# Divisors of the first batch: from matmuls against the identity to a round trip through DRAM, with the division placed by slot

## Chip, cores, metric

One NeuronCore of a Trainium2 chip. The metric is device time of one execution in microseconds. The kernel before takes 1337.45 us, the median of three runs (1337.2 to 1339.41).

## What is computed

Threshold attention over 8 batches of 8 heads, 576 tokens and head size 64, whose output is the input of a two-layer MLP with an exact GELU, in float32:

```python
scores = scale * np.matmul(q, k.transpose(0, 1, 3, 2))
thresh = np.max(scores, axis=-1, keepdims=True) - tau
scores = np.where(scores >= thresh, scores, -1000000000.0)
scores = scores - np.max(scores, axis=-1, keepdims=True)
attn = np.exp(scores)
attn = attn / (np.sum(attn, axis=-1, keepdims=True) + 1e-09)
...
x = np.ascontiguousarray(attn_out.transpose(0, 2, 1, 3)).reshape(B * S, H * D)
h = x @ w_in                                   # 4608 x 512 by 512 x 2048
g = 0.5 * h * (1.0 + erf(h * inv_sqrt2))
out = g @ w_out                                # 4608 x 2048 by 2048 x 512
```

The kernel does not divide the probabilities. It weighs V with the undivided ones and divides the result x^T (features on partitions, tokens along the row) by the sum of each token's row. The divisor belongs to a token, which is a partition where the sum is made and a column where x^T is divided, so the sums have to be transposed, and repeated over the 64 feature rows of each head. How that is done in the first batch is what the change replaces.

## The kernel before

**Slots.** The order of work is written out by hand: one loop (line 1086) runs over slots `(p, i)`, p a pair of heads, i a chunk of 128 query tokens (i = 4, called NC, is the tail of 64 tokens of both heads together). The first batch is pairs 0 to 3 ("early"), in 20 slots: n = 0 to 7 are chunks 0 and 1 of pairs 0, 1, 2, 3; n = 8 to 10 are chunks 2, 3 and NC of pair 0, n = 11 to 13 those of pair 1, 14 to 16 of pair 2, 17 to 19 of pair 3. From n = 20 (BATCH) on, seven more batches follow with five slots a pair. After them a part on the last ten blocks of 256 tokens ends the program.

**A slot of the first batch** issues, in this order: the scores (TensorE, line 408); `softmax_head`: maxima (VectorE, 420), thresholds `thr` (GpSimd, 423), exponentials (ScalarE, 425); additions of converted weights that have become due (GpSimd, 224); what is due from earlier slots: V weighed (TensorE, 544 or 568; copied to x^T by ScalarE, 554 or 570) and the division; MLP matmuls (`fill`, 636 and 651), as many as a written goal for this slot allows, from n = 10 on; the transposes of the slot before (TensorE 354, copied by ScalarE 361 and 370, for NC 365 and 374); `softmax_tail`: threshold applied and row sums made (VectorE 441). Then come loads and a share of the conversion of the MLP weights (ScalarE 202 and 203, VectorE 210 and 211), which is spread over n = 0 to 19. Each engine carries out its own instructions strictly in that order, so one that waits holds up all behind it. The scores have two PSUM buffers, each free again when line 441 has read it.

**Weights.** They arrive in 32 pieces of 512 KB, issued on the queue of SyncE (SP, line 183). A new piece is issued as a conversion frees a buffer; eight are issued before the first conversion. The SP queue also issues the loads of q, k and v of pairs 4 and 5 (lines 258 and 267) at n = 13 and n = 17. `w_out_sb[15]` to `w_out_sb[12]` are filled by the last four pieces.

**The division in the first batch.** `softmax_tail` gives each slot its own tile of sums, `den`, adds 1e-9 to it on GpSimd (444) and VectorE inverts it a slot later (450). `divide_early`, called right after the V-weighing of the tokens concerned, transposes and repeats the inverses with matmuls: the column of inverses, repeated 64 times, is the stationary side and the identity the moving one (463). ScalarE copies the result out of PSUM (465), and GpSimd multiplies x^T with it (471). It is called eight times: for tokens 0 to 255 of pairs 0 to 3 in n = 3, 5, 7, 9, for tokens 256 to 575 in n = 12, 15, 18, 21. The first MLP matmuls, in n = 10, read tokens 0 to 255 of all four pairs, one pair per value of c, in the order c = 0, 1, 2, 3.

**Later batches** do it otherwise (`divisors`, 473): the sums of a pair stand in the columns of one tile `sums`, are inverted and transposed by VectorE (482), written to DRAM (485) and read back repeated over 64 partitions (491 and 493), and `divide` multiplies (584).

Of the kernel before, what the change touches and what calls it, by code (L numbers as in the profile page):

```python
# [8 lines left out]
FP32 = mybir.dt.float32  # L9
# [3 lines left out]
ALU = mybir.AluOpType  # L13
# [5 lines left out]
def kernel(  # L19
# [40 lines left out]
    TAIL = S - MAIN  # L60
# [4 lines left out]
    N_DF = d_ff // P  # L65
    TOK = 256
# [6 lines left out]
    SLOTS = NC + 1  # L73
# [13 lines left out]
    w_out_sb = [w_out_all[:, j, :] for j in range(N_DF)]  # L87
# [5 lines left out]
    dg = late_end.enter_context(tc.tile_pool(name="dg", bufs=1))  # L93
# [27 lines left out]
    ident = const.tile([P, P], FP32, name="ident")  # L121
# [8 lines left out]
    sums = [att.tile([P, Q], FP32, name=f"sums{i}") for i in range(2)]  # L130
# [111 lines left out]
    st = {}  # L242
# [156 lines left out]
    def scores(p, i):  # L399
        s = st[p]  # L400
        n = 1 if i == NC else 2
        sc = s["sc", i] = [ps.tile([P, 2, 512], FP32, tag="sc", name="sc", bufs=2) for _ in range(n)]
        for h in range(2):
            for e in range(n):
                rows = slice(0, P) if i == NC else slice(e * D, (e + 1) * D)
                lhsT = s["q_tail"] if i == NC else s["qT"][rows, i * P:(i + 1) * P]
                at = h * HALF + (TAIL if p < EARLY and e == 0 else 0)
                nc.tensor.matmul(  # L408
                    sc[e][:, h, 0:HALF], lhsT=lhsT, rhs=s["kT"][rows, at:at + HALF], start=True, stop=True)

    def softmax_head(p, i):

        s = st[p]
        n = len(s["sc", i])
        nmx = small.tile([P, 2], FP32, tag="nmx", name="nmx")
        thr = s["thr", i] = small.tile([P, 2], FP32, tag="thr", name="thr")
        w = s["p", i] = work.tile([P, 2 * S], FP32, tag="p", name="p")
        for e in range(n):
            sc = s["sc", i][e][:, :, 0:HALF]
            nc.vector.tensor_reduce(nmx[:, e:e + 1], sc, axis=AXIS.XY, op=ALU.max, negate=True)  # L420
            if e == 0:
                add_low_bits(True)
            nc.gpsimd.tensor_scalar(  # L423
                thr[:, e:e + 1], nmx[:, e:e + 1], -1.0, tau_eff, op0=ALU.mult, op1=ALU.subtract)
            nc.scalar.activation(  # L425
                w[:, e * S:(e + 1) * S].rearrange("p (h s) -> p h s", h=2), sc, AF.Exp, bias=nmx[:, e:e + 1], scale=1.0)

    def softmax_tail(p, i):

        s = st[p]  # L430
        sc, thr, w = s.pop(("sc", i)), s.pop(("thr", i)), s["p", i]
        n = len(sc)
        if p < EARLY:
            pair = small.tile([P, 2], FP32, tag="den", name="den", bufs=2 * SLOTS)
            den = [pair[:, e:e + 1] for e in range(n)]
        else:
            at = [e * NC + i if i < NC else 2 * NC for e in range(n)]
            den = [sums[p % 2][:, x:x + 1] for x in at]
        for e in range(n):
            row = w[:, e * S:(e + 1) * S].rearrange("p (h s) -> p h s", h=2)  # L440
            nc.vector.scalar_tensor_tensor(  # L441
                row, sc[e][:, :, 0:HALF], thr[:, e:e + 1], row, op0=ALU.is_ge, op1=ALU.mult, accum_out=den[e])
        if p < EARLY:
            nc.gpsimd.tensor_scalar(pair[:, 0:n], pair[:, 0:n], 1e-9, None, op0=ALU.add)
            s["sum", i] = pair[:, 0:n]

    def invert(p, i):

        den = st[p]["sum", i]
        nc.vector.reciprocal(den, den)  # L450

    def divide_early(p, lo, hi):


        s = st[p]
        b, hp = divmod(p, HP)
        tr = ps.tile([P, 512], FP32, tag="mm", name="tr")
        for i in range(lo // P, -(-hi // P)):
            den = s.pop(("sum", i))
            to = tr[:, i * P - lo:min((i + 1) * P, hi) - lo]  # L460
            for e in range(2):
                one_of, cols = (den[:, e:e + 1], ident) if i < NC else (den, ident[:, e * TAIL:(e + 1) * TAIL])
                nc.tensor.matmul(to[e * D:(e + 1) * D, :], lhsT=one_of.to_broadcast([P, D]), rhs=cols, start=True, stop=True)
        by = dg.tile([P, S], FP32, tag="inv", name="inv")
        nc.scalar.copy(by[:, 0:hi - lo], tr[:, 0:hi - lo])
        for n, o, at, size in in_blocks(b, lo, hi):
            x, y = x_blk[n][:, hp, o:o + size], by[:, at - lo:at - lo + size]
            if size == TOK:
                x = x.rearrange("q (p c) -> q c p", c=2)
                y = y.rearrange("q (c p) -> q c p", c=2)  # L470
            nc.gpsimd.tensor_tensor(x, x, y, op=ALU.mult)

    def divisors(p):
# [98 lines left out]
    def in_blocks(b, lo, hi):  # L572
        while lo < hi:
            n, o = divmod(b * S + lo, TOK)
            size = min(TOK - o, hi - lo)
            yield n, o, lo, size
            lo += size
# [498 lines left out]
    PARTS = 1.3, 1.3, 0.2, 1.3, 0.9  # L1076

    HALVED = (2, 3)
    BUSY = {1: 2, 6: 2, 8: 2, BATCH: 4}

    tokens = 0
# [4 lines left out]
    for n in range(len(slots) + WEIGH + 1):  # L1086
        p, i = slots[n] if n < len(slots) else divmod(n, SLOTS)
        early = p < EARLY
        last = slots[n - 1] if 0 < n <= len(slots) else None
        if p < NP:  # L1090
            scores(p, i)
            softmax_head(p, i)
            add_low_bits()
            if last and last[0] < EARLY:
                invert(*last)
            if p < HP - 1 and i == 0:
                turn_qk_early(p + 1)
        elif n == len(slots):
            early_end.close()
            weights_first()  # L1100
# [4 lines left out]
        for args in due:  # L1105
            if len(args) == 2:
                weigh_half(*args)
                if args[1]:
                    divide_early(args[0], 0, TOK)
                continue  # L1110
            weigh_v(*args)
            divide_early(*args)
        due = []
        if p > EARLY and i == WEIGH:
            for lo, hi in (0, WIDE), (WIDE, S):
# [10 lines left out]
        if p < NP:  # L1126
            softmax_tail(p, i)
# [92 lines left out]
```

## Time and profile before

| what | value |
|---|---|
| median of three runs | 1337.45 us |
| the profiled execution's own time | 1338.74 us |
| its span, first to last instruction | 1336.9 us |
| busy: TensorE, VectorE, GpSimd, ScalarE | 99%, 78%, 47%, 45% of the span |
| granted TensorE clock | 0.998 |
| first batch (n = 0 to 19) | up to 127.76 us, where the scores of n = 20 start |
| matmuls of line 463 | 80, 272 ns at the median |
| copies of line 465 | 8, 421 ns at the median |
| reciprocals of line 450 | 20, 155 ns at the median |
| additions of line 444 | 20, 276 ns at the median |
| multiplications of line 471 | 12, 742 ns at the median |

How to read the lines below. A line of the timeline has the start in us from the beginning of the span, the duration in us, the engine (PE is TensorE, PEld its weight load, DVE VectorE, ACT ScalarE, POOL GpSimd, SPq the queue of SyncE), the line of the source, the operation, output and inputs with their shape, and how many instructions were merged; the bracket has the idle time of the engine ahead of it and what ended it. A float32 matmul is two instructions in the trace. Their ends are modelled and overlap by some 0.1 us, so what a group costs TensorE is read from starts: from its first instruction to the start of what follows.

A slot n is found by its scores (line 408). They start at 30.06 (n = 4), 36.14 (5), 41.83 (6), 47.86 (7), 52.48 (8), 59.24 (9), 63.87 (10), 69.04 (11), 74.29 (12), 84.18 (13), 89.28 (14), 93.78 (15), 102.53 (16), 107.63 (17), 113.13 (18), 123.12 (19), 127.76 (20), 131.64 (21) and 141.35 us (22).

### The profile page before, as it was taken

Reading aid. Unit: us, or ns where it says so; the run is one execution under the profiler, and the core shown is the slowest. Engines: PE = TensorE matmul, PEld = TensorE weight load, DVE = VectorE, ACT = ScalarE, POOL = GpSimd, SP = SyncE. Lnnn points to the kernel's source line nnn. Section 1 sums busy time; section 2 is a strip of 40 time slices with the busy share of each in tenths; the row PEclk is TensorE's granted clock in tenths of the full one; section 3 lists DMA queues with packets and bytes.
Section 4 is the critical chain, followed back from the end, with each engine's and each line's share of the span. In section 5 each row is a group of like instructions: output and inputs, shape, how many; then the busy total and the mean of one; then the engine's idle time right before and its main releaser. Section 6 shows DMA issues by size and latency. Waiting matters only on the chain.

```text
span 1336.9 us, 19969 instructions
## 1 busy us (share of the span) xinstructions
PE 1318.9 (99%) x6362; PEld 893.4 (67%) x6362; DVE 1038.9 (78%) x2005; ACT 605.4 (45%) x1029; POOL 633.6 (47%) x1061
## 2 busy tenths in 40 slices
PE   8899999999999999999999999999999999999998
PEld 6677466466466466457556557568787787877877
DVE  6877777788888888888888888783857698386775
ACT  7987457268367358338438438322211113211120
POOL 3655454555555555545546551245264503635530
PEclk9999999999999999999999999999999999999999
DMA  8553566776776786786787775400000130000003
GB/s 258 196 150 62 124 151 141 167 183 153 175 188 153 179 201 153 180 209 155 165 219 164 164 187 124 106 9 1 1 0 1 40 101 18 0 1 0 1 0 79
DMA packets 209784, 152.42 MB, mean 114 GB/s; under 512 B 113360, under 2 KB 193088, under 8 KB 209680
## 3 DMA queue, kind: packets, MB, share of 16 engines
q1 hardware_dynamic: 192256, 127.21, 40.1%
q0 software_dynamic: 16992, 23.64, 6.7%
q8 instruction: 52, 0.85, 0.3%
q14 instruction: 52, 0.43, 0.1%
q10 hardware_dynamic: 432, 0.30, 0.1%
HBM read 55.97 MB, written 12.52 MB: 51 GB/s over the span
## 4 chain that ended last, share of the span: by engine, by line
PE 92%; DVE 2%; ACT 2%; DMA 2%; SPq 1%; issue 1%; POOL 0%; ACTq 0%; DVEq 0%
PE bank L824 34%; PE o_ps L651 17%; PE hT L636 16%; PE sc L408 13%; PE xT L544 11%; ACT p L425 1%; DVE nmx L420 1%; DMA q<-in_q_dram 1%; PE tr L354 1%; DMA x<-xall 1%; DVE power L211 1%; DMA turned_p<-in_moe_w_in_dram 0%; ACT pT L361 0%; DVE p L441 0%; DVE power L210 0%
## 5 line engine op out<-in xcount | busy, mean ns | idle before, releaser
L425 ACT ACTIVATE p<-sc,nmx 128x576 f32<-128x576 f32 x288 | 201.8, 737 | 272.7 <-DVE nmx L420 272.2
L441 DVE SCALAR_TENSOR_TENSOR p<-sc,thr,p 128x576 f32<-128x576 f32 x288 | 225.3, 816 | 74.8 <-ACT p L425 65.1
L423 POOL TENSOR_SCALAR thr<-nmx,tau_eff 128x1 f32<-128x1 f32 x288 | 83.9, 293 | 341.9 <-DVE nmx L420 337.6
L636 PE MATMUL hT<-xall,w_in 128*128 128x256 f32 x1024 | 242.0, 386 | 0.5 <-ACT g L603 0.5
L420 DVE TENSOR_REDUCE nmx<-sc 128x1 f32<-128x576 f32 x288 | 205.4, 750 | 44.5 <-PE sc L408 43.1
L651 PE MATMUL o_ps<-w_out,g 128*128 128x512 f32 x512 | 236.8, 603 | 0.0
L636 PEld LDWEIGHTS hT<-xall,w_in 128*128 128x128 f32 x1024 | 189.3, 190 | 50.8 <-issue 23.0
L706 DVE TENSOR_TENSOR c<-c,bank 128x320 f32<-128x320 f32 x304 | 146.7, 487 | 34.2 <-PE bank L824 21.0
L706 DVE TENSOR_TENSOR o<-o,bank 128x256 f32<-128x256 f32 x240 | 99.8, 419 | 93.7 <-PE bank L824 88.7
L651 PEld LDWEIGHTS o_ps<-w_out,g 128*128 128x128 f32 x512 | 93.1, 190 | 109.2 <-issue 106.8
L408 PE MATMUL sc<-kT,qT 64*128 64x288 f32 x960 | 159.9, 431 | 2.1 <-DVE p L441 1.6
L544 PE MATMUL xT<-pT,v 128*64 128x320 f32 (+1 forms) x1240 | 159.9, 411 | 0.6 <-DVE pT L365 0.5
L505 DVE STREAM_TRANSPOSE turned_p<-p 128x1152 f32<-128x1152 f32 x112 | 154.4, 1378 | 3.9
L408 PEld LDWEIGHTS sc<-kT,qT 64*128 64x128 f32 x960 | 91.0, 186 | 75.8 <-issue 60.1
L544 PEld LDWEIGHTS xT<-pT,v 128*64 128x64 f32 x1240 | 86.7, 137 | 71.9 <-issue 11.3
L824 PE MATMUL bank<-w_out,c 128*128 128x256 f32 x480 | 120.2, 381 | 0.5 <-DVE o L706 0.5
L267 POOL DMA_DIRECT2D v<-in_v_dram x208 | 110.8, 536 | 4.3 <-issue 2.1
L824 PEld LDWEIGHTS bank<-w_out,c 128*128 128x128 f32 x480 | 89.9, 190 | 18.8 <-DVE o L706 3.0
L877 ACT ACTIVATE c<-c 128x320 f32<-128x320 f32 (+1 forms) x80 | 46.9, 623 | 114.6 <-DVE c L706 114.5
L824 PE MATMUL bank<-t_out,c 128*128 128x256 f32 x320 | 82.8, 381 | 0.0
L706 POOL TENSOR_TENSOR c<-c,g 128x320 f32<-128x320 f32 (+1 forms) x40 | 50.5, 1271 | 67.5 <-DVE c L706 67.5
L824 PE MATMUL bank<-t_out,g 128*128 128x256 f32 x320 | 82.1, 379 | 0.0
(180 smaller groups left out, 1757.7 us busy)
## 6 DMA issues: line engine op xcount, KB each, us to landing
pT<-turned_p SPq DMA_DIRECT2D x448, 160.0 KB, 3.5
pT<-pd_tail SPq DMA_DIRECT2D x112, 80.0 KB, 2.7
q<-in_q_dram POOLq DMA_DIRECT2D x104, 72.0 KB, 3.7
k<-in_k_dram POOLq DMA_DIRECT2D x104, 72.0 KB, 3.1
inv<-turned SPq DMA_DIRECT2D x54, 128.0 KB, 4.0
v<-in_v_dram POOLq DMA_DIRECT2D x156, 40.0 KB, 3.1
out_dram<-o SPq DMA_DIRECT2D x40, 128.0 KB, 2.3
xall<-in_moe_w_out_dram SPq DMA_DIRECT2D x9, 512.0 KB, 4.1
```

The costliest lines, as they stand in the source:

```text
L267: eng.dma_start(t[r:P:4, e, 0:n, :], rows[:, r * KR:r * KR + n, :])
L408: nc.tensor.matmul(sc[e][:, h, 0:HALF], lhsT=lhsT, rhs=s["kT"][rows, at:at + HALF], start=True, stop=True)
L420: nc.vector.tensor_reduce(nmx[:, e:e + 1], sc, axis=AXIS.XY, op=ALU.max, negate=True)
L423: nc.gpsimd.tensor_scalar(thr[:, e:e + 1], nmx[:, e:e + 1], -1.0, tau_eff, op0=ALU.mult, op1=ALU.subtract)
L425: nc.scalar.activation(w[:, e * S:(e + 1) * S].rearrange("p (h s) -> p h s", h=2), sc, AF.Exp, bias=nmx[:, e:e + 1], scale=1.0)
L441: nc.vector.scalar_tensor_tensor(row, sc[e][:, :, 0:HALF], thr[:, e:e + 1], row, op0=ALU.is_ge, op1=ALU.mult, accum_out=den[e])
L505: nc.vector.transpose(turned_p[:, :, i // 2, 0:NB, i % 2 * Q:(i % 2 + 1) * Q], w.rearrange("p (e b i) -> p e b i", e=2, i=Q))
L544: nc.tensor.matmul(to, lhsT=s["v"][:, e, c, :], rhs=rhs, start=(c == 0), stop=(c == KR - 1))
L636: nc.tensor.matmul(hT[:, j % 2, :], lhsT=w_in_sb[c][:, j * P:(j + 1) * P], rhs=x_blk[n][:, c, :], start=(c == 0), stop=(c == N_DM - 1))
L651: nc.tensor.matmul(o[:, 0:d_model], lhsT=g[j][:, m * P:(m + 1) * P], rhs=w_out_sb[j], start=(j == 0), stop=(j == N_DF - 1))
L706: eng.tensor_tensor(out, a, b, op=ALU.add)
L824: nc.tensor.matmul(to, lhsT=l, rhs=r, start=start and k == 0, stop=k == len(pairs) - 1, skip_group_check=not start)
```

## The change

The first batch gets its divisors as the later ones do. `softmax_tail` writes the sums of early pairs into columns of `sums[p % 2]` too. After chunk 1 and after NC of a pair GpSimd adds 1e-9 to all nine columns at once. A slot later, at n = 2, 4, 6, 8 (tokens 0 to 255 of pairs 0 to 3) and n = 11, 14, 17, 20 (tokens 256 to 575), the new `divisors_early` inverts the nine columns and transposes the tile on VectorE, writes it to DRAM and reads it back repeated, all on the SP queue. For tokens 0 to 255 the target is `w_out_sb[15 - p]`, which the MLP weights fill later; for the rest it is the tile `inv`, of which there is one. `divide_early` is left with the multiplication on GpSimd. For tokens 256 to 575 it stays where it was (n = 12, 15, 18, 21); for tokens 0 to 255 of pairs 0, 1, 2, 3 it is now in n = 5, 7, 9, 10, after what is due in that slot and ahead of `fill`. Its columns are read in another order (4 x 2 x 32 in place of 2 x 128).

```diff
@@ softmax_tail
-        if p < EARLY:
-            pair = small.tile([P, 2], FP32, tag="den", name="den", bufs=2 * SLOTS)
-            den = [pair[:, e:e + 1] for e in range(n)]
-        else:
-            at = [e * NC + i if i < NC else 2 * NC for e in range(n)]
-            den = [sums[p % 2][:, x:x + 1] for x in at]
+        at = [e * NC + i if i < NC else 2 * NC for e in range(n)]
+        den = [sums[p % 2][:, x:x + 1] for x in at]
...
-        if p < EARLY:
-            nc.gpsimd.tensor_scalar(pair[:, 0:n], pair[:, 0:n], 1e-9, None, op0=ALU.add)
-            s["sum", i] = pair[:, 0:n]
-
-    def invert(p, i):
-        den = st[p]["sum", i]
-        nc.vector.reciprocal(den, den)
+        if p < EARLY and i in (1, NC):
+            at = sums[p % 2][:, 0:2 * NC + 1]
+            nc.gpsimd.tensor_scalar(at, at, 1e-9, None, op0=ALU.add)
+
+    def divisors_early(p, i):
+        den = sums[p % 2]
+        nc.vector.reciprocal(den[:, 0:2 * NC + 1], den[:, 0:2 * NC + 1])
+        turned = small.tile([P, Q], FP32, tag="turned", name="turned", bufs=2)
+        nc.vector.transpose(turned, den)
+        rows = dram.tile([4, Q, Q], FP32, tag="turned", name="turned", bufs=4)
+        nc.sync.dma_start(rows.rearrange("a k i -> (a k) i"), turned)
+        t = w_out_sb[N_DF - 1 - p] if i == 1 else dg.tile([P, S], FP32, tag="inv", name="inv")
+        st[p]["inv", i] = t
+        flat = rows.rearrange("a k i -> a (k i)")
+        c = 0 if i == 1 else 2
+        for e in range(2):
+            to = t[e * D:(e + 1) * D]
+            src = flat[:, (e * NC + c) * Q:(e * NC + c + 2) * Q].unsqueeze(0).to_broadcast([D, 4, 2 * Q])
+            nc.sync.dma_start(to[:, 0:TOK].rearrange("p (a x) -> p a x", x=2 * Q), src)
+            if i == NC:
+                src = rows[2 * e:2 * e + 2, 2 * NC, :].unsqueeze(0).to_broadcast([D, 2, Q])
+                nc.sync.dma_start(to[:, TOK:TOK + TAIL].rearrange("p (a x) -> p a x", x=Q), src)
@@ divide_early
-        tr = ps.tile([P, 512], FP32, tag="mm", name="tr")
-        for i in range(lo // P, -(-hi // P)):
-            den = s.pop(("sum", i))
-            to = tr[:, i * P - lo:min((i + 1) * P, hi) - lo]
-            for e in range(2):
-                one_of, cols = (den[:, e:e + 1], ident) if i < NC else (den, ident[:, e * TAIL:(e + 1) * TAIL])
-                nc.tensor.matmul(to[e * D:(e + 1) * D, :], lhsT=one_of.to_broadcast([P, D]), rhs=cols, start=True, stop=True)
-        by = dg.tile([P, S], FP32, tag="inv", name="inv")
-        nc.scalar.copy(by[:, 0:hi - lo], tr[:, 0:hi - lo])
+        by = st[p].pop(("inv", 1 if lo == 0 else NC))
...
-                x = x.rearrange("q (p c) -> q c p", c=2)
-                y = y.rearrange("q (c p) -> q c p", c=2)
+                x = x.rearrange("q (a i c) -> q a c i", i=Q, c=2)
+                y = y.rearrange("q (a c i) -> q a c i", i=Q, c=2)
             nc.gpsimd.tensor_tensor(x, x, y, op=ALU.mult)
@@ the loop over slots
+    DIVIDE_EARLY = {5: 0, 7: 1, 9: 2, 10: 3}
...
-            if last and last[0] < EARLY:
-                invert(*last)
+            if last and last[0] < EARLY and last[1] in (1, NC):
+                divisors_early(*last)
...
                 weigh_half(*args)
-                if args[1]:
-                    divide_early(args[0], 0, TOK)
                 continue
             weigh_v(*args)
-            divide_early(*args)
+            if args[1]:
+                divide_early(*args)
+        if n in DIVIDE_EARLY:
+            divide_early(DIVIDE_EARLY[n], 0, TOK)
         due = []
```

More of the change, by code (lines that the diff above doesn't have):

```diff
@@ L442, in softmax_tail @@
                 row, sc[e][:, :, 0:HALF], thr[:, e:e + 1], row, op0=ALU.is_ge, op1=ALU.mult, accum_out=den[e])
-        if p < EARLY:
-            nc.gpsimd.tensor_scalar(pair[:, 0:n], pair[:, 0:n], 1e-9, None, op0=ALU.add)
-            s["sum", i] = pair[:, 0:n]
-    def invert(p, i):
-        den = st[p]["sum", i]
-        nc.vector.reciprocal(den, den)
+        if p < EARLY and i in (1, NC):
[19 more added lines that the diff above has]
+                nc.sync.dma_start(to[:, TOK:TOK + TAIL].rearrange("p (a x) -> p a x", x=Q), src)
     def divide_early(p, lo, hi):
-        s = st[p]
         b, hp = divmod(p, HP)
-        tr = ps.tile([P, 512], FP32, tag="mm", name="tr")
-        for i in range(lo // P, -(-hi // P)):
-            den = s.pop(("sum", i))
-            to = tr[:, i * P - lo:min((i + 1) * P, hi) - lo]
-            for e in range(2):
-                one_of, cols = (den[:, e:e + 1], ident) if i < NC else (den, ident[:, e * TAIL:(e + 1) * TAIL])
-                nc.tensor.matmul(to[e * D:(e + 1) * D, :], lhsT=one_of.to_broadcast([P, D]), rhs=cols, start=True, stop=True)
-        by = dg.tile([P, S], FP32, tag="inv", name="inv")
-        nc.scalar.copy(by[:, 0:hi - lo], tr[:, 0:hi - lo])
+        by = st[p].pop(("inv", 1 if lo == 0 else NC))
         for n, o, at, size in in_blocks(b, lo, hi):
```

## The prediction

> **What bounds the kernel now.** I began with the page's chain that ended last: TensorE holds 92% of it. Then a table by stage (columns: stretch, its length, busy us and instruction count of PE, PEld, DVE, ACT, POOL, granted clock, DMA share, GB/s) shows where that isn't so.
>
> ```profile
> PE 92%; DVE 2%; ACT 2%; DMA 2%; SPq 1%; issue 1%; POOL 0%; ACTq 0%; DVEq 0%
> ```
>
> ```profile
> 0.00:64.00 64.00, 55.37 (x504) 40.78 (x505) 47.92 (x113) 52.57 (x110) 30.88 (x56) 0.97 0.73 233
> ...
> 113.00:123.00 10.00, 9.25 (x62) 6.18 (x63) 7.42 (x17) 7.23 (x17) 5.27 (x10) 1.00 0.14 31
> ...
> 141.50:160.00 18.50, 18.50 (x60) 8.90 (x61) 14.90 (x28) 4.13 (x7) 11.69 (x24) 1.00 0.71 157
> ```
>
> Up to 64 us TensorE has 8.6 us of idle time, so its work there is not simply the bound; in n = 10 to 21 it is nearly so; from n = 22 on it never idles. A shift gained or lost by 141 us therefore goes through to the end. All of the change lies ahead of that. So the timeline of n = 9 to 17 was read next, for who waits for whom.
>
> ```profile
> 61.56 0.61 PE L463 MATMUL tr<-ident,den 128*64 128x128 f32 x8
> ...
> 64.41 0.74 POOL L471 TENSOR_TENSOR xall<-xall,inv 128x256 f32<-128x256 f32 x1
> ...
> 64.95 3.19 PE L636 MATMUL hT<-xall,w_in 128*128 128x256 f32 x14
> ...
> 66.24 1.27 POOL L224 TENSOR_TENSOR w_in<-power,w_in 128x512 uint32<-128x512 uint32 x1 [0.72 <-DVE power L211]
> ...
> 67.49 0.30 POOL L423 TENSOR_SCALAR thr<-nmx,tau_eff 128x1 f32<-128x1 f32 x1
> ...
> 68.61 1.07 ACT L361 COPY pT<-tr 128x512 f32<-128x512 f32 x2 [1.00 <-PE tr L354]
> ```
>
> See that GpSimd finishes pair 3's division at 65.15, 1.1 us ahead of its first use: the fourth MLP matmul, at 64.95 + 3 x 0.43 = 66.24 (pitch 0.43: seven from 64.95 to 67.97). And that ScalarE waits for TensorE's transposes right after.
>
> ```profile
> 102.24 1.07 ACT L361 COPY pT<-tr 128x512 f32<-128x512 f32 x2 [2.17 <-PE tr L354]
> ...
> 105.38 1.27 POOL L224 TENSOR_TENSOR w_out<-power,w_out 128x512 uint32<-128x512 uint32 x1 [3.34 <-DVE power L211]
> ...
> 106.63 0.30 POOL L423 TENSOR_SCALAR thr<-nmx,tau_eff 128x1 f32<-128x1 f32 x1
> ...
> 106.96 0.82 DVE L441 SCALAR_TENSOR_TENSOR p<-sc,thr,p 128x576 f32<-128x576 f32 x1 [0.99 <-POOL thr L423]
> ...
> 107.63 1.45 PE L408 MATMUL sc<-pd_tail,qT 64*128 64x288 f32 x8
> ```
>
> Here, in n = 16 and 17, VectorE waits for a GpSimd threshold, and TensorE's scores for VectorE (107.71, end of the first part of line 441). GpSimd itself had idled 3.34 us. Last, the SP queue, and what divisors through DRAM cost in later batches:
>
> ```profile
> 86.46 0.33 SPq L183 DMA_DIRECT2D xall<-in_moe_w_out_dram  x1
> 86.84 2.13 SPq L258 DMA_DIRECT2D q<-in_q_dram  x4
> 89.14 3.08 SPq L258 DMA_DIRECT2D k<-in_k_dram  x4
> 92.33 5.03 SPq L267 DMA_DIRECT2D v<-in_v_dram  x8
> 97.46 0.52 SPq L183 DMA_DIRECT2D turned_p<-in_moe_w_out_dram  x1
> ...
> 164.56 0.57 SPq L485 DMA_DIRECT2D turned<-turned  x1
> 166.57 0.60 SPq L491 DMA_DIRECT2D inv<-turned  x1
> ```
>
> SP is taken up for 11 us in n = 13 to 15 by pair 4's loads; and the reading back is issued 2.0 us after the writing.
>
> [...] 16 KB to DRAM lands after 1.9 us at the median (1.8 to 2.9), the reads after 3.9 (3.4 to 5.7, line 491). [...] of two 512 KB pieces issued 0.63 us apart (97.46, 98.09) one lands after 4.0 us, the other after 5.0. [...] line 210 takes 0.96 us at 64.47 in place of 0.42 while line 471 runs. [...]
>
> **The change, part by part.** Signed costs on the path, in us.
>
> *TensorE.* 80 matmuls go. From first start to what follows, four groups take 0.54 each (61.56 to 62.10 in n = 9; n = 3, 5, 7 alike), four 0.65 to 0.9 (78.91 to 79.56 in n = 12; n = 15, 18, 21). *ScalarE* loses eight copies of 0.42.
> - n = 3: line 361 starts at 29.68, waiting for TensorE. Without line 463 (28.56 to 29.00) and line 465, it can start when line 554 (from 28.69, 0.40) and four transposes are done, 29.25: **-0.43**. n = 5: likewise 41.44 to 40.91, **-0.53**.
> - n = 7 and 9: **0**. VectorE's chain is unbroken from 43.3 to 67: line 211 ends (49.87), line 224 takes 1.27 from 50.02, then thr, then line 441 at 51.60, 1.8 us in every slot.
> - n = 12: TensorE is on the path (ScalarE waits 3.06 for it): **-0.65**. n = 15 the same: **-0.65**.
> - n = 18: TensorE idles 0.45 for ScalarE's line 603. The built program now makes these matmuls wait on TensorE alone, since a PSUM tile fewer is in turn; the next bound is line 603's end at 120.6, for transposes that started at 121.62. I take **-0.6** (0 to -1.0).
> - n = 21: scores of n = 22 start at 141.35; VectorE's line 441 frees the second of their two buffers at 141.09, and the second of four matmuls (0.29 each) needs it, so they start near 140.8: **-0.5**.
>
> *VectorE.* 20 reciprocals go, 8 and 8 transposes (0.21, line 482) come. The pair takes 0.37 and fits into the 0.48 us ahead of line 441 in which it waits for thr anyway; in n = 14 and 20 it overhangs by 0.1, under slack of 0.3 and 0.5. **0**. *GpSimd* makes 12 additions fewer, none on the path; the new column order of the multiplication is not in the trace: 0.74, at most 1.0 each. **0**, 0.26 above in n = 10.
>
> *Weights behind the new SP traffic.* SP stands 2 to 5 us at each write. Pieces land 8 us or more ahead of use after the first six (piece 9: issued 26.9, used 47.7), so **0**; without that cover each us would be a us. Pair 4's loads are ahead of it; pair 5's move from 102 to about 119 and are used at 140.6.
>
> *Division of pair 3 in n = 10.* It now stands behind line 224 and thr of that slot: start 67.77, end 68.5, and the fourth MLP matmul waits for it from 66.24. Queued behind: three MLP matmuls, the transposes, ScalarE's copies, line 202, line 210, maxima of n = 11. All that was tight (ScalarE waited 1.00). **+2.35** (2.3 to 2.6). The other three are done where or before the old ones were.
>
> *Division of pair 1, tokens 256 on, in n = 15.* By then the sum is +0.74 (n = 13). Its five DMAs stand behind pair 4's 16 loads and a 512 KB piece: write issued at 98.05 + 0.74 = 98.8. [...] it lands near 102.0, after 3.2 us. The reads go out at 102.1, 102.7, 103.4, 104.0; the third, the last that the larger multiplication needs, lands at 107.3, the fourth at 107.9. Multiplications end at 108.4 (0.74 and 0.32), line 224 at 109.7, thr at 110.0. Without that, thr would end at 106.93 + 0.09 = 107.0. VectorE's line 441 and TensorE's scores of n = 17 wait: **+3.0**. Lower bound: 1.9 to land and 3.4 to read, 1.1. Upper: reads of 5.9, 4.8. Pair 0's reads (n = 12) land near 83, GpSimd's next work is at 87; pairs 2 and 3 (n = 18, 21) are in before their turn.
>
> Sum: -0.43 - 0.53 + 2.35 - 0.65 - 0.65 + 3.0 - 0.6 - 0.5 = **+2.0**. The profiled execution (span 1336.9, own time 1338.74) would become 1338.9 and 1340.7; it lies 1.29 above the median of the runs, to which I apply the same +2.0: **1339.4**.
>
> **Rivals.** A measurement can tell about 0.2%, 2.7 us, from no change.
> 1. *Main case*: both waits, second one 1.1 to 3.7: 1337.5 to 1340.1. Chance 0.45.
> 2. *Slower*: the reads for pair 1 land past 108.7; from there the sum exceeds 2.7. For it: a piece in front, [...] landings of up to 5.9 seen. Against: nothing issued behind them. At 4.8 it gives 1341.2. Chance 0.33.
> 3. *Second wait absent*: needs the reads in by 104.4, sooner than any seen: -1.0, 1336.4. Chance 0.05.
> 4. *Faster*: the first is covered too, or taken up by idle time of TensorE in n = 12 to 18 (0.67, 0.29, 0.24, 0.45): 1336.4 - 2.35 = 1334.1. Against: these gaps are ends of chains through TensorE itself. Chance 0.12.
> 5. *It doesn't do what it says*: SP's stops starve the conversion after all; some 3 us more than case 1, 1342.4. Chance 0.05.
>
> Faster by over 0.2% has 0.12 (case 4), slower 0.38 (2 and 5), within it 0.50. The range leaves out case 5, most of case 4 and the top of 2: 1335.5 to 1341.6; the main case's own is 1337.5 to 1340.1.
>
> **What would show it.** Line 463 gone; in n = 10 a TensorE gap of 2.3 us ended by GpSimd's multiplication; in n = 15 GpSimd idle until a DMA, and VectorE's wait for thr in n = 16 grown from 1.0 to about 4; scores of n = 22 starting near 143.3. It is wrong if either gap is missing, if ScalarE waits for a weight piece, or if line 441 waits in n = 12, 18 or 21.

## Result and the profile after

The changed kernel takes **1351.99 us**, the median of four runs (1351.79 to 1354.53); the kernel before takes 1337.38 (four runs). The ratio is 1.0116, its 95% interval 1.0103 to 1.0129. The profiled execution has a span of 1350.1 us, 13.2 more than before. The forecast was 1339.4, its range ended at 1341.6. (A single run can fall into a slower state of the chip: one of the 13 of the last experiment took 1512.13 us at a granted clock of 0.85 and is left out of its median.)

The page's chain that ended last, after the change. TensorE had 92% of it before and has 88% now; DMA has gone from 2% to 4%:

```profile
PE 88%; DMA 4%; DVE 3%; SPq 2%; ACT 1%; issue 1%; POOL 1%; DVEq 0%; ACTq 0%; POOLq 0%
```

The table by stage of the changed kernel (columns as before the change: stretch, its length, busy us and instruction count of PE, PEld, DVE, ACT, POOL, granted clock, DMA share, GB/s):

```profile
64.00:80.00 16.00, 6.68 (x24) 5.28 (x22) 3.49 (x7) 1.64 (x3) 2.52 (x4) 0.69 0.47 169
...
153.50:172.00 18.50, 18.50 (x60) 8.89 (x58) 14.90 (x28) 4.80 (x7) 12.30 (x24) 1.00 0.67 143
```

Of the kernel before, the stretch of the first row:

```profile
64.00:80.00 16.00, 15.31 (x94) 11.24 (x95) 13.53 (x29) 13.37 (x29) 9.38 (x15) 1.00 0.56 170
```

This is the news: in 64 to 80 us TensorE works 6.68 us in place of 15.31, and its clock is at 0.69 in place of 1.00. The last row of the changed kernel is n = 22, in which TensorE is full as it was. So the loss lies ahead of it. To place it, the start of each slot's scores (line 408) was compared, after minus before:

| slot n | 2 | 4 | 6 | 10 | 11 | 12 | 13 | 15 | 16 | 17 | 18 | 19 | 21 | 22 | 24 on |
|---|---|---|---|---|---|---|---|---|---|---|---|---|---|---|---|
| shift, us | -0.56 | -1.08 | -1.52 | -1.06 | +11.22 | +11.09 | +10.53 | +10.54 | +10.02 | +10.02 | +13.59 | +13.04 | +13.07 | +12.53 | +12.9 |

Two steps lose much: n = 10 to 11, **+12.28**, and n = 17 to 18, **+3.57**. (n = 2, 9 and 22 lose some 0.36 each.) The timeline of n = 10 after the change:

```profile
63.25 0.75 POOL L476 TENSOR_TENSOR xall<-xall,w_out 128x256 f32<-128x256 f32 x1
63.85 1.46 PE L641 MATMUL hT<-xall,w_in 128*128 128x256 f32 x6
65.15 1.26 POOL L224 TENSOR_TENSOR w_in<-power,w_in 128x512 uint32<-128x512 uint32 x1 [1.15 <-DVE power L211]
66.39 0.29 POOL L423 TENSOR_SCALAR thr<-nmx,tau_eff 128x1 f32<-128x1 f32 x1
...
73.84 0.73 POOL L476 TENSOR_TENSOR xall<-xall,w_out 128x256 f32<-128x256 f32 x1 [7.16 <-DMA w_out<-turned]
74.63 3.78 PE L641 MATMUL hT<-xall,w_in 128*128 128x256 f32 x8 [9.32 <-POOL xall L476]
78.20 2.13 PE L354 MATMUL tr<-ident,p 128*128 128x128 f32 x9
```

GpSimd is through with line 224 and the threshold at 66.7, as forecast, and then waits 7.16 us for a DMA: pair 3's divisors. TensorE waits 9.32 us for GpSimd. (Matmuls are counted here and below by their instructions in the trace, two to a matmul of the source; a transpose is one. So the 80 of line 463 are 40 matmuls of the source.) Then its eight matmuls take 3.78 us and nine transposes 2.13; the same take 1.99 and 1.15 where the clock is at 1.00 (kernel with division first, below). 9.32 + 1.79 + 0.98 is 12.1 of the 12.28.

Why the divisors are late is told by SP's queue in the changed kernel (line 453 is the write, 461 the reads, 183 a piece of weights):

```profile
46.67 0.54 SPq L183 DMA_DIRECT2D turned_p<-in_moe_w_in_dram  x1
47.32 0.37 SPq L183 DMA_DIRECT2D xall<-in_moe_w_in_dram  x1
47.82 0.35 SPq L183 DMA_DIRECT2D turned_p<-in_moe_w_in_dram  x1
48.27 0.77 SPq L453 DMA_DIRECT2D turned<-turned  x1
55.58 1.25 SPq L461 DMA_DIRECT2D w_out<-turned  x2
56.94 0.54 SPq L183 DMA_DIRECT2D xall<-in_moe_w_out_dram  x1
57.58 0.37 SPq L183 DMA_DIRECT2D turned_p<-in_moe_w_out_dram  x1
58.05 0.37 SPq L183 DMA_DIRECT2D xall<-in_moe_w_out_dram  x1
58.53 0.40 SPq L183 DMA_DIRECT2D turned_p<-in_moe_w_out_dram  x1
59.02 0.60 SPq L453 DMA_DIRECT2D turned<-turned  x1
67.57 1.25 SPq L461 DMA_DIRECT2D w_out<-turned  x2
```

SP stands from a write until it lands, since the reads behind it need it: pair 3's lands at 67.56, its reads go out at 67.57. Meanwhile conversions free buffers, and when SP is let go, three pieces, then four go out in a row, some 0.5 us apart. The kernel before sent them two to a slot here, 1.05 us apart or more:

```profile
54.83 0.33 SPq L183 DMA_DIRECT2D xall<-in_moe_w_out_dram  x1
55.89 0.33 SPq L183 DMA_DIRECT2D turned_p<-in_moe_w_out_dram  x1
60.28 0.33 SPq L183 DMA_DIRECT2D xall<-in_moe_w_out_dram  x1
61.33 0.33 SPq L183 DMA_DIRECT2D turned_p<-in_moe_w_out_dram  x1
```

Pair 3's write is issued right behind its four pieces and lands after 8.5 us, 0.17 us after the last of them. From write to reads it is 5.5, 4.8, 7.3, 8.5 us for pairs 0 to 3.

The second loss, n = 15 to 17 after the change:

```profile
116.67 1.02 POOL L476 TENSOR_TENSOR xall<-xall,inv 128x256 f32<-128x256 f32 x2 [6.16 <-DMA inv<-turned]
117.65 1.27 POOL L224 TENSOR_TENSOR w_out<-power,w_out 128x512 uint32<-128x512 uint32 x1
118.90 0.30 POOL L423 TENSOR_SCALAR thr<-nmx,tau_eff 128x1 f32<-128x1 f32 x1
119.23 0.82 DVE L437 SCALAR_TENSOR_TENSOR p<-sc,thr,p 128x576 f32<-128x576 f32 x1 [3.31 <-POOL thr L423]
120.11 1.23 PE L408 MATMUL sc<-pd_tail,qT 64*128 64x288 f32 x6 [1.71 <-DVE p L437]
121.27 4.97 PE L641 MATMUL hT<-xall,w_in 128*128 128x256 f32 x14
```

GpSimd's order holds its next work up: the threshold's maxima are there at 115.91, but it starts at 118.90, behind the wait of 6.16 us and line 224. This is the forecast chain, but its last row isn't: 14 matmuls of the MLP take 4.97 us, and took 3.29 before.

### The profile page after: what moved, and what is told of

It is laid out like the page before. It is cut to its first block, busy times and chain, and to the rows that moved or that the text cites. A ratio compares the mean times of both kernels' runs of the same rounds, so it can differ in the third digit from the quotient of the medians.

```text
span 1350.1 us, 19850 instructions
## 1 busy us (share of the span) xinstructions
PE 1321.2 (98%) x6282; PEld 893.1 (66%) x6282; DVE 1039.2 (77%) x2001; ACT 603.5 (45%) x1021; POOL 629.5 (47%) x1049
## 3 DMA queue, kind: packets, MB, share of 16 engines
q0 software_dynamic: 16992, 23.64, 6.8%
## 4 chain that ended last, share of the span: by engine, by line
PE 88%; DMA 4%; DVE 3%; SPq 2%; ACT 1%; issue 1%; POOL 1%; DVEq 0%; ACTq 0%; POOLq 0%
PE bank L829 34%; PE o_ps L656 16%; PE hT L641 15%; PE sc L408 12%; PE xT L549 10%; DMA turned<-turned 1%; PE tr L354 1%; DVE p L437 1%; DMA x<-xall 1%; DVE nmx L420 1%; ACT p L425 1%; DMA turned_p<-in_moe_w_in_dram 0%; DMA w_out<-turned 0%; DVE power L210 0%; DVE power L211 0%
## 5 line engine op out<-in xcount | busy, mean ns | idle before, releaser
L641 PE MATMUL hT<-xall,w_in 128*128 128x256 f32 x1024 | 245.5, 389 | 9.3 <-POOL xall L476 9.3
L711 POOL TENSOR_TENSOR c<-c,g 128x320 f32<-128x320 f32 (+1 forms) x40 | 50.5, 1272 | 67.5 <-DVE c L711 67.5
```

The lines of the kernel that those rows point to most:

```text
L641: nc.tensor.matmul(hT[:, j % 2, :], lhsT=w_in_sb[c][:, j * P:(j + 1) * P], rhs=x_blk[n][:, c, :], start=(c == 0), stop=(c == N_DM - 1))
L711: eng.tensor_tensor(out, a, b, op=ALU.add)
```

## Experiments

Three theories were put to the test. **Theory 1**: SP, held at each landing, lets freed pieces pile up, and the next write lands behind their burst. **Theory 2**: the way through DRAM is long in itself. **Theory 3**: the place of pair 3's division in GpSimd's order decides. "Step" is the growth of the shift against the kernel before from the start of one slot's scores to the next; it is cleaner than the total (see the end of this part). Every kernel starts from the changed one unless said otherwise; its line numbers differ from the changed kernel's by what the edit adds.

**Reads a slot later.** The write stays, the first half's reads are issued in the next slot.

```diff
         nc.sync.dma_start(rows.rearrange("a k i -> (a k) i"), turned)
+        st[p]["rows"] = rows
+        if i == NC:
+            read_divisors(p, i)
+
+    def read_divisors(p, i):
+        rows = st[p].pop("rows")
...
+            if n > 1 and slots[n - 2][0] < EARLY and slots[n - 2][1] == 1:
+                read_divisors(*slots[n - 2])
```

> The changed kernel, but the reads of the first half's divisors are issued one slot after the write, so that SP doesn't stand still at the write's landing. Theory 1 (SP held at each landing lets freed pieces pile up, and the next write lands behind their burst): the pieces go out singly, each write lands in some 2 to 4 us, pair 3's reads are in by 66, the wait of n = 10 shrinks from 9.3 us to about 2 (the division still stands behind GpSimd's other work), total about 1342. Theory 2 (the way through DRAM is long in itself): the reads come a slot later still, the wait of n = 10 stays at 9 us or grows, total 1352 or more. Theory 3 (where the division stands in GpSimd's order decides): unchanged, 1352.

Measured: 1343.29 us, ratio 1.0047 (1.0032 to 1.0062). The step of n = 10 falls from 12.28 to 4.04. Its timeline (write 453, reads 467, division 482):

```profile
57.10 0.33 SPq L453 DMA_DIRECT2D turned<-turned  x1
...
59.81 0.33 SPq L183 DMA_DIRECT2D xall<-in_moe_w_out_dram  x1
...
60.87 0.33 SPq L183 DMA_DIRECT2D turned_p<-in_moe_w_out_dram  x1
...
61.28 1.25 SPq L467 DMA_DIRECT2D w_out<-turned  x2
...
67.71 0.73 POOL L482 TENSOR_TENSOR xall<-xall,w_out 128x256 f32<-128x256 f32 x1
...
68.49 3.67 PE L647 MATMUL hT<-xall,w_in 128*128 128x256 f32 x8 [2.12 <-POOL xall L482]
```

The pieces go out no more than two in a row again, and pair 3's write lands after 3.1 us (8.5). The reads, a slot later in the order, go out 6.3 us earlier (61.28, not 67.57). Theories 2 and 3 fall as the main cause. (SP is not quite free: for pairs 1 and 2 it still stands at the landing, after 6.3 and 4.9 us, but then no burst of three or four follows.) Of the step left, 2.12 us are the wait for a division that starts right behind the threshold, 1.9 us after its reads have landed; the other 1.7 us are the eight matmuls, 3.67 in place of 1.99.

**Reads without a wait.** The first half's reads take a tile of ones written at the start, so SP is never held by these writes; tokens 0 to 255 of the first batch are divided by wrong numbers.

```diff
+        if i == 1:
+            rows = ones_rows
```

> The changed kernel, but the reads for tokens 0 to 255 take a DRAM tile of ones that was written once at the start, so they don't wait for the write just ahead of them; the writes stay. Left out: tokens 0 to 255 of the first batch are divided by the wrong numbers. All instructions and transfers are otherwise the same. Theory 1: SP is never held, no bursts, wait of n = 10 about 2 us, total about 1341 to 1342. Theory 2, if it is the reads that are slow: 1350 or more; if it is the landing of the write: as theory 1, but pieces bunched as now. Theory 3: 1352.

Measured: 1345.21 us, ratio 1.0061 (1.0046 to 1.0076); step of n = 10 4.05, again a wait of 2.12 us and eight matmuls in 3.63. The instructions and bytes are those of the changed kernel but for the one write of the ones, yet the reads wait for no landing: 8.2 us of the 12.28 go with that. This kernel takes away the whole wait for the landing, and not only SP's hold; that it is the hold is shown by the kernel with the reads a slot later, whose divisors do come through DRAM and whose step is the same (4.04). The total is 3 to 4 us above its expectation: the eight slow matmuls weren't in it (1.7), and the step of n = 17 is 5.26 in place of 3.57 (see the second half).

**The write on ScalarE's queue.**

```diff
-        nc.sync.dma_start(rows.rearrange("a k i -> (a k) i"), turned)
+        (nc.scalar if i == 1 else nc.sync).dma_start(rows.rearrange("a k i -> (a k) i"), turned)
```

> The changed kernel, but the first half's writes are issued by ScalarE into its own queue; the reads stay with SP. Theory 1: [...] lands in 2 to 3 us, so SP is held shortly and the wait of n = 10 falls to 2 to 5 us; against it stand four issues on ScalarE of about 0.4 us each: total 1342 to 1346. If the pieces slow the write by sharing the DMA engines and DRAM [...], the write still takes 5 us or more and the total stays near 1350. Theory 3: 1352 or more.

Measured: 1349.77 us, ratio 1.0100 (1.0083 to 1.0117). For pair 3 it is 3.4 us from write (63.59) to reads (67.01), and the step of n = 10 is **2.36**; the forecast was 2.35. The expectation of the total was wrong, for another reason: the step of n = 2 is +6.0.

```profile
74.97 1.99 PE L641 MATMUL hT<-xall,w_in 128*128 128x256 f32 x8 [2.12 <-POOL xall L476]
```

```profile
26.96 0.35 ACTq L453 DMA_DIRECT2D turned<-turned  x1
27.36 0.69 ACT L327 ACTIVATE qT<-tr,q_scale 128x512 f32<-128x512 f32 x1 [5.36 <-DMA xall<-in_moe_w_in_dram]
28.09 0.93 PEld L354 LDWEIGHTS tr<-ident,p 128*128 128x128 f32 x5 [7.25 <-ACT qT L327]
```

ScalarE itself stood 5.36 us at the issue until a piece had landed. The semaphores in the trace explain it: in this program the DMAs of SP and ScalarE take eight in turn, and the write waits for the DMA that had the same one eight issues before, a piece issued at 22.46 and landed at 26.88. Moving a DMA to a busy engine's queue moved such a wait there too.

**SP held again, all else repaired.** The reads are issued at the end of the slot of the write, ahead of that slot's new pieces, pair 3's division stands first in n = 10, and the second half's division a slot later.

```diff
-            if n > 1 and slots[n - 2][0] < EARLY and slots[n - 2][1] == 1:
-                read_divisors(*slots[n - 2])
...
+        if last and last[0] < EARLY and last[1] == 1:
+            read_divisors(*last)
```

> All divisors through DRAM, with three repairs: the first half's reads are issued at the end of the slot in which the write is issued (ahead of that slot's new pieces), pair 3's division stands first in n = 10, and the second half's division for pairs 0 to 2 stands one slot later. If the three causes found are all there is, no step loses more than 0.4 and the gains remain (n = 5 -0.44, n = 12, 15, 18, 21 together -2.2): about 1334.5, 3 us below the kernel before. If holding SP at the landing in itself brings the bursts back, n = 10 costs several us again and the total is 1340 or more.

Measured: 1346.27 us, ratio 1.0066 (1.0051 to 1.0080). It was meant as the best version, and the case named last in its expectation came: writes take 5.9, 7.1 and 7.9 us again, the step of n = 10 is 7.83.

```profile
53.34 0.54 SPq L183 DMA_DIRECT2D xall<-in_moe_w_out_dram  x1
53.98 0.37 SPq L183 DMA_DIRECT2D turned_p<-in_moe_w_out_dram  x1
54.45 0.38 SPq L183 DMA_DIRECT2D xall<-in_moe_w_out_dram  x1
54.93 0.37 SPq L183 DMA_DIRECT2D turned_p<-in_moe_w_out_dram  x1
56.23 0.33 SPq L453 DMA_DIRECT2D turned<-turned  x1
64.13 1.25 SPq L467 DMA_DIRECT2D w_out<-turned  x2
```

Reads moved by less than a slot bring the burst of four and the late landing back. Theory 1 holds in both directions.

**The bursts alone.** Only the second half is divided by way of DRAM; the first half's writes and reads are issued, but TensorE turns its divisors as before the change.

```diff
-                invert(*last)
+                divisors_early(*last)
...
     def divisors_early(p, i):
+        if i == 1:
+            invert(p, i)
```

(Shown against the kernel with the second half alone, below. `invert` keeps a copy of the inverted sums, which TensorE then turns; what the DMAs bring is not used.)

> The kernel with only the second half through DRAM (+2.27 us at n = 22 by its profile, +3.9 by its median), and the first half's writes and reads issued as in the changed kernel, but not used: TensorE turns these divisors as before. Left out is nothing of the computation. SP is held at each landing and the pieces come in bursts. If the conversion of the weights has the slack that the prediction gave it (0 for this step), n = 10 costs nothing and no step differs by more than 0.5 from the kernel without these transfers: 1338 to 1342. If the held pieces starve the conversion, ScalarE waits for them and some slots up to n = 12 lose 1 us or more each.

Measured: 1344.80 us, ratio 1.0054 (1.0035 to 1.0073). SP's queue shows the same bursts (57.98 to 59.57, write 60.03, reads 67.88), and n = 10 and 11 lose nothing by them: their steps are 0.00 and 0.01. So the conversion of the weights has the slack the prediction gave it. (n = 14 and 15 together lose 0.56 against the kernel with the second half alone; why stays open.) The total is above the expected range; by the slots the kernel is at +3.6 until 584 us, and the rest (5.5, in the profiled execution) comes between 585 and 710 us, which this part's end takes up.

**Division first.** On the kernel with the reads a slot later, pair 3's division is moved ahead of line 224 and the threshold in n = 10.

```diff
+        if n == 10:
+            divide_early(3, 0, TOK)
         if p < NP:
             scores(p, i)
...
-        if n in DIVIDE_EARLY:
+        if n in DIVIDE_EARLY and n < 10:
```

> The kernel with the reads a slot later, and pair 3's division placed first among GpSimd's work of n = 10 (ahead of that slot's line 224 and threshold) instead of last. With the reads a slot later, the step from n = 10 to 11 cost 4.04: a wait of 2.12 us for the multiplication and 1.8 us in which eight MLP matmuls ran at 0.50 of the clock. If the place of the division in GpSimd's order is what is left (the term of +2.35), the wait falls to the arrival of the reads (issued 61.28 and 61.9, landing after 4.1, so near 66.0, multiplied by 66.8, needed at 66.4): 0.4 us or less, no fall of the clock, step of 0 to +0.6, and the time falls by 3.5 to 4. If the reads are what is late, the step stays at 3 to 4.

Measured: 1342.12 us, ratio 1.0033 (1.0021 to 1.0045); step 1.71 in place of 4.04. Half a hit: the place in GpSimd's order matters, but then the reads are what ends last. They land near 66.6, not 66.0, and TensorE waits 1.47 us, with no fall of the clock:

```profile
66.75 0.74 POOL L482 TENSOR_TENSOR xall<-xall,w_out 128x256 f32<-128x256 f32 x1 [2.00 <-DMA w_out<-turned]
...
67.54 1.99 PE L647 MATMUL hT<-xall,w_in 128*128 128x256 f32 x8 [1.47 <-POOL xall L482]
69.37 1.15 PE L354 MATMUL tr<-ident,p 128*128 128x128 f32 x9
```

Theory 3 names part of what is left behind theory 1; the last 1.5 us are theory 2's, the length of the way itself.

**TensorE kept busy.** On the same kernel, 16 matmuls of no use stand ahead of the matmul that waits.

```diff
+                if n == 0 and j == 0 and c == 3:
+                    keep_busy(4)
```

> The kernel with the reads a slot later, and 16 matmuls of no use (about 2.3 us) ahead of the fourth MLP matmul of n = 10, so that TensorE is not idle while it waits for pair 3's division. If the fall of the clock after a wait is a cost of its own, the clock stays at 1.00, the eight matmuls behind the wait take 1.85 us in place of 3.67, and the step from n = 10 to 11 falls from 4.04 to about 2.4. If those matmuls are slow for another reason (operands, DMA traffic), the step stays at 4 or grows by what the filling exceeds the wait.

Measured: 1345.29 us, ratio 1.0054 (1.0038 to 1.0069). The total did not fall (1343.29 without the filling), but the step did what was expected, 2.37 in place of 4.04:

```profile
66.18 1.95 PE L304 MATMUL idle<-ident 128*128 128x128 f32 x16
...
68.47 1.99 PE L649 MATMUL hT<-xall,w_in 128*128 128x256 f32 x8 [0.35 <-POOL xall L482]
```

The division ends at the same time as without the filling (68.4), and the eight matmuls take 1.99 us in place of 3.67. The fall of the clock is a cost of its own, 1.7 us here.

**Second half alone, and pair 1's place in SP's queue.** First only tokens 256 on go through DRAM.

```diff
-            if last and last[0] < EARLY and last[1] in (1, NC):
+            if last and last[0] < EARLY and last[1] == 1:
+                invert(*last)
+            if last and last[0] < EARLY and last[1] == NC:
                 divisors_early(*last)
```

> Only tokens 256 on go through DRAM; tokens 0 to 255 are turned by TensorE and copied by ScalarE where they were before. All three theories put the 12.3 us of n = 10 on the first half, so it must go; the steps of n = 12, 15, 16/17, 18 and 21 must stay as in the changed kernel (-0.56, -0.52, +3.57, -0.55, -0.54, together +1.4): 1338.8 us, 1.4 above the kernel before. If the time stays near 1352, or lies below 1337, the steps don't add up and the shift by slot is no sum of causes.

Measured: 1341.51 us (12 runs, 1337.61 to 1345.05), ratio 1.0025 (1.0015 to 1.0035). The 12.28 go, n = 12, 15, 18 and 21 keep their gains (-0.56, -0.52, -0.55, -0.54); n = 17 costs 5.06 in place of 3.57. There the clock falls for longer, 6.8 us in place of 3.4: six matmuls of the scores take 2.28 us (1.23 in the changed kernel) behind a wait of 2.04. The run with the clock at 1.000 in the mean is the one of 1337.61, the one at 0.996 that of 1345.05.

Two repairs of this kernel. Division of pairs 0 to 2 a slot later:

```diff
             weigh_v(*args)
+            if args[1] and args[0] < EARLY - 1:
+                then.append(args)
+                continue
             divide_early(*args)
```

(`then` is worked off in the next slot behind the exponentials and additions of weights.)

> Only tokens 256 on go through DRAM, and the division for pairs 0 to 2 stands one slot later in GpSimd's order (pair 3's where it was). If the cost of n = 15 to 17 is the wait of GpSimd for the reads with line 224 and the threshold of n = 16 queued behind (measured 5.06 us with its fall of the clock in the kernel with only this half), it goes altogether; the gains of n = 12, 15, 18 and 21 (-0.56, -0.52, -0.55, -0.54) remain: 2 to 3 us below the kernel before, 1335.0. If the wait moves on with the division to n = 17 or 18, the time stays near 1340.

Measured: 1340.38 us, ratio 1.0016 (1.0005 to 1.0027). GpSimd no longer waits for the reads and the step of n = 17 is 0.71, but n = 14 costs 0.40 and in n = 15 the gain of -0.52 becomes +0.08, presumably since the multiplications now stand in GpSimd's way a slot later. Most of the cost goes, not all of it. The total missed the 1335 expected; this profile's scores of n = 0 start 1.7 us late, too. And pair 4's 16 loads behind pair 1's divisors:

```diff
-        if p == 1 and i == NC:
-            load(HP)
...
                 divisors_early(*last)
+            if last == (1, NC):
+                load(HP)
```

> Only tokens 256 on go through DRAM, as in the kernel with only this half (whose steps n = 15 to 17 cost 5.06 net), and SP issues pair 4's 16 loads behind the divisors of pair 1 instead of ahead of them. If those divisors are late because they queue behind the loads, they arrive before n = 15 needs them, the wait of GpSimd (6 us) goes, the 5.06 goes, and n = 12, 15, 18 and 21 keep their -0.5 each: 2 to 3 us below the kernel before, 1335, unless pair 4's q is now late for its scaling in n = 17. If the way through DRAM is late without the loads too, at least 1 to 3 us of the 5.06 stay and the time is 1337 or more.

```profile
91.65 0.33 SPq L459 DMA_DIRECT2D turned<-turned  x1
93.48 0.59 SPq L467 DMA_DIRECT2D inv<-turned  x1
...
96.08 2.21 SPq L258 DMA_DIRECT2D q<-in_q_dram  x4
```

Measured: 1337.53 us, ratio 1.0001 (0.9993 to 1.0009). From write to reads it is 1.8 us, GpSimd multiplies at 99.22 without a wait, and the step of n = 17 is 0.16. So pair 1's divisors were late because they stood behind the loads and the piece. The total is 2.5 us above the 1335 expected, though by the slots this kernel is at -2.0 us from n = 24 on (-0.5 of it ahead of n = 0).

**All repairs together.** The edits of three kernels above, in one: reads a slot later, pair 3's division first, loads behind pair 1's divisors; all divisors through DRAM.

> All divisors through DRAM, reads of the first half a slot later, pair 3's division first in n = 10 (together 1.71 left of 12.28 at that step), and pair 4's loads behind pair 1's divisors. If the three causes are separate, the step at n = 16 and 17 (3.94 there) goes as well: from 1342.1 to about 1338.3, level with the kernel before. If one repair undoes another, it stays above 1340.

Measured: 1336.55 us (12 runs), ratio 0.9995 (0.9987 to 1.0003). Steps of 1.22 in n = 10 and 0.02 in n = 17: the causes are separate. And with pair 3's first half left to TensorE, in the old place of its division:

```diff
-            if last and last[0] < EARLY and last[1] in (1, NC):
+            if last == (EARLY - 1, 1):
+                invert(*last)
+            elif last and last[0] < EARLY and last[1] in (1, NC):
                 divisors_early(*last)
...
                 weigh_half(*args)
+                if args == (EARLY - 1, 1):
+                    divide_early(args[0], 0, TOK)
...
-        if n in DIVIDE_EARLY:
+        if n in DIVIDE_EARLY and n < 10:
```

> Divisors through DRAM except for pair 3's first half, which TensorE turns as before; first half's reads a slot later; pair 4's loads behind pair 1's divisors. By the causes found no wait is left: n = 10 costs 0, n = 16 and 17 cost 0, and the gains of n = 5 (-0.44), 12, 15, 18 and 21 (-0.5 to -0.56 each) remain: 1334.5 to 1335.5, about 2.5 us below the kernel before. If it lies above 1337.4, a cost was overlooked that the other kernels hid.

Measured: 1337.27 us (12 runs), ratio 0.9997 (0.9989 to 1.0005); steps 0.38 and 0.00. The 1335 expected was missed. By the slots these two are at -3.1 and -2.2 us from n = 24 on, of which -0.9 and 0.0 lie ahead of n = 0 already; in the total neither can be told from the kernel before. Their profiles, one execution each, lose 1.0 and 1.4 us of it between 585 and 755 us. **What stays open**: there TensorE's wait differs from profile to profile. Near 590 us, where ScalarE waits for a buffer that is being written to DRAM (3.94 us in the kernel before), TensorE waits 1.07 us in the kernel before, 2.06 and 1.68 in these two, and 2.34 in the kernel with the bursts alone, there followed by 3.4 us at half the clock. Whether a shift of the first batch changes these waits in the mean was not tried. The kernel before alone spreads from 1334.8 to 1340.7 in 35 runs.

## Why the prediction was wrong, point by point

- **"Division of pair 3 in n = 10", +2.35: the step that failed; measured 12.28.** It took line 224 and the threshold as all that the division waits for. With the reads in time just that is measured (2.36 in the kernel with the write on ScalarE's queue, the same wait of 2.12 in two others). The landing of these reads was never worked out, though it was for pair 1's in n = 15. Ready 56.03, written 59.02, landed 67.5, read 67.57 to 68.8, used 73.84: the same sum, with 3.0 us until the write is issued and 8.5 until it lands, gives the wait. Moving the reads a slot later, so that no burst stands ahead of the write, took 8.2 of the 12.28 away.
- **"Weights behind the new SP traffic", 0**: true of the weights (bursts alone: n = 10 and 11 lose nothing). But "SP stands 2 to 5 us at each write" was too small (4.8 to 8.5), and the question stopped at who waits for the pieces. It had to go on: what do pieces that are held back collide with when they are let go? With the next write. Rival 5 named SP's stops, but had the conversion starve; the divisors did.
- **TensorE's clock, nothing charged for it**: wrong. It is 2.8 us of n = 10 and 1.7 of n = 17. That waits such as those forecast cost no clock was the author's estimate, and the trace before already spoke against it: its clock is at 0.50 from 23.64 to 27.05 us, and TensorE's only wait in the 3.4 us ahead of that took 1.53 us (21.1 to 22.6). Half clock came behind a wait of 2.12 us in two kernels and not in a third; the last part sets them side by side.
- **"Division of pair 1, tokens 256 on, in n = 15", +3.0; measured 3.57**: mechanism right, terms not. The write to reads took 3.3 us (forecast 3.2, the author's estimate; the write landed at 111.81, the piece ahead of it at 111.60), third read to multiplication 3.5 (3.9), so the threshold ended 2.25 us late, not 3.0, and TensorE lost 1.9 of the 3.57 by the wait; 1.7 are the clock (14 matmuls in 4.97 us, not 3.29). VectorE's wait for the threshold grew from 0.99 to 3.31 us (forecast: about 4). Two errors that nearly cancel: that 3.57 lies near 3.0 is luck. Its cause, the loads ahead in SP's queue, is shown by their move.
- **n = 12, 15, 18, 21** (-0.65, -0.65, -0.6, -0.5): -0.56, -0.52, -0.55, -0.54. But of the last, 0.37 is given back in n = 22: its scores start earlier and then take 1.54 us in place of 1.17, up to the next matmul, the second of their buffers being free no sooner. All 13 kernels that have the change, whole or in part, show these 0.37. **n = 5** (-0.53): -0.44, and 0.00 in the kernel that keeps TensorE's turn in n = 5. **n = 7 and 9** (0): +0.10 and +0.35; the latter is there without the first half's change too, unexplained. **n = 3** (-0.43): n = 2 and 3 together show -0.52. The kernel with the second half alone, which keeps these matmuls, shows -0.97, but only because its clock doesn't fall near 24 us, as it does in the kernel before and in the changed one. Like against like, the matmuls are worth 0.4: with the fall, -0.03 where they are kept (two kernels) and -0.41 to -0.52 where they are gone (five); without it, -0.97 to -0.99 (two) and -1.40 to -1.43 (three). The forecast holds.
- **VectorE and GpSimd, 0**: right; the multiplication in its new order takes 0.73 to 0.75 us (0.74 before).

## What to carry to other kernels

A wait that was put into a shared DMA queue had two prices here: what stood behind it was late (SP stood 7.3 us at pair 2's write), and what had gathered behind it left in one burst (four pieces) and was ahead of the next small transfer (pair 3's write, 8.5 us; 1.4 with nothing else under way). So issue the dependent transfer only when what it needs has landed. For every consumer of a moved result write the whole chain down, source, issue, landing, issue, landing, use, and not only the one that looks tight. A stall of TensorE of 1 to 2 us should be priced with and without a halved clock behind it: behind 2.12 us, eight matmuls took 3.67 us in one kernel here and 1.99 in another.

## What the hardware showed beyond expectation

**The clock.** Granted clock of the kernel with the reads a slot later, by the us (columns: stretch, length, busy of PE, clock, DMA share, GB/s):

```profile
67.00:68.00 1.00, 0.00 (x0) 1.00 0.76 188
68.00:69.00 1.00, 0.51 (x1) 0.76 0.83 332
69.00:70.00 1.00, 1.00 (x4) 0.50 0.01 4
...
72.00:73.00 1.00, 1.00 (x10) 1.00 0.49 197
```

The clock falls when the wait (66.4 to 68.5) ends and work begins, and is back after 3.4 us. In the kernel with the write on ScalarE's queue a wait of the same 2.12 us leaves it at 1.00. In the changed kernel it falls 4.8 us into the wait of 9.32 (at 70.11) and returns 5.7 us after work has resumed (at 80.35).

The times at which the clock changes tell the two apart. In all 14 traces the stretch from one change to the next is a whole multiple of 3.413 us. In the changed kernel they are 17.07, 3.41, 27.31, 3.41, 13.65, 10.24, 40.96, 3.41 and 1225.39 us, so 5, 1, 8, 1, 4, 3, 12, 1 and 359 times; in the kernel before 17.07, 3.41 and 1307.31, so 5, 1 and 383 times. Windows of that length, counted from the changes, are used below. In the kernel above, the wait lies wholly in one window (65.10 to 68.51), and the next is at half clock; on ScalarE's queue the border at 74.67 cuts the wait into 1.83 and 0.29 us. TensorE's idle time by window in the 14 traces, as far as the modelled ends of its matmuls tell:

- **Down**: of the windows at full clock, all 12 with 1.9 us or more of idle time were followed by one at half clock, 16 of 56 with 1.1 to 1.9 us, and none of 5320 with less. In between the idle time alone doesn't decide: in the changed kernel a window with 1.12 us (from 49.63) was followed by half clock, one with 1.38 us (from 63.28) was not. What else does is open.
- **Up**: half clock ended only behind a window in which TensorE was never idle (26 of 26, four of them in the changed kernel); all 8 with idle time, 0.16 us or more, were followed by another, in the changed kernel those with 3.41 and 1.11 us (from 70.11 and 73.52). With this agrees that a wait of 2.04 us comes with 6.8 us at half clock in the kernel with the second half alone: 0.93 us of it reaches into the first slow window (107.40 to 110.81).

**A small write behind large reads.** With nothing else under way, 16 KB to DRAM land after 1.4 us (23 writes of the first batch's divisors in the 13 kernels, 1.41 to 1.44). The other 68 were issued while earlier transfers were under way, and 64 of them landed 0.15 to 0.29 us after the last of these (the remaining four 0.4 to 1.5 us after). So such a write was as late as what was ahead of it: 3.1 us behind two pieces of 512 KB, 7.3 behind three and two reads, 8.5 behind four and two reads. The queue made no difference: the four writes on ScalarE's queue landed 0.16 to 0.22 us after SP's last piece.
